# Output projection of a gated MLP as a stage of its own, with one level of Strassen's scheme over pairs of token tiles

## The chip, the cores and the metric

The kernel runs on one core of one Trainium2 chip. The metric is the device time of one execution in microseconds (us); the median of several runs is given, and one further execution was recorded by the hardware profiler. The engines are called PE (TensorE), DVE (VectorE), ACT (ScalarE), POOL (GpSimd) and SP (SyncE); PEld is TensorE's loading of weights.

## What is computed

One layer over 2048 tokens of 640 features: sliding-window attention with a residual, and then a gated MLP with a residual. The MLP is what matters here; with h the result of the attention part, it is

```python
F = w_in.shape[-1]; Fh = F // 2                      # F = 1728, Fh = 864
z = _gelu(jnp.einsum("bsd,df->bsf", _layernorm(h), w_in))
z1 = z[..., :Fh]
z2 = _layernorm(z[..., Fh:], axis=-1)
g = jnp.einsum("ts,bsf->btf", w_sp, z2) + b_sp[None, :, None]
h2 = h + jnp.einsum("bsf,fd->bsd", z1 * g, w_out)    # w_out is 864 x 640
```

The spatial gate `w_sp @ z2` multiplies a 2048 x 2048 matrix with 2048 x 864; the output projection multiplies 2048 x 864 with 864 x 640. All is float32 in and out.

## The kernel before

A token tile has 128 tokens, so there are 16 tiles. A feature row of 864 is seen as two halves of 432 (`HF`), or as seven blocks of 128 (`KF`; the seventh has 96); an output row of 640 as two halves of 320 (`HD`). Float32 accuracy comes from splitting each operand into a high and a low part (fp32r): `split` writes the high part by a copy on ACT (L140) and the low part by a subtraction on DVE (L141), and each product is three matmuls, high by high, high by low, low by high.

The stages follow each other: layer norm and QKV, attention, `wo` with the residual (h goes to `h_d`), z1 (`z_pair`, results to `z1_d`), the first half of z2, the first half of the spatial gate, the second half of z2, the second half of the gate, and within the latter the output projection.

The gate works on pairs of token tiles p and p+8 (`gate_pair`, L1076), as one level of Strassen's scheme (Winograd's form with shared sums): two tiles by two halves of the contracted tokens on one side, by two feature halves of 432 on the other. The seven products are called B11, T1, T2, B22, T3, B21, T4; each is 4 blocks by 3 matmuls of 432 columns (L1136), 84 in a pair. `first_gate` does it with the first half of the contracted tokens and stores the partial sums to `g_d`. `second_gate` (L1223) loads those back, adds the products (L797, `row<-g`) and then forms z1·(g+b) by one scalar_tensor_tensor a half tile (`gated`, L1237) in one of two buffers for z1, into which z1 was loaded from `z1_d` (L1240).

The output projection takes one tile at a time: `turn_y` transposes the gated tile in seven pieces on PE (L1190) into two PSUM banks, from where ACT and DVE split it into `y_sp`; `project` (L1196) multiplies with the split `w_out` (7 blocks by 3 by 2 halves = 42 matmuls of 320 columns, L1201); `final_half` adds h and stores. During `second_gate(p)` the two tiles of pair p-1 are done, behind the gate's products 0 to 3 (`turns`, `extra`); the last two tiles come after the loop (L1371 to L1378). `w_out` is loaded and split in `second_gate(0)` (`load_wout`, `put_wout`).

The order: `steps` is a list of (PE part, what follows it) and `at(n, f)` hangs a preparation on step n; `run` walks through them. That gives the order of the program and by it the dependences. From step 62 on (L1361) no order by hand holds any more, and a list scheduler sets the order of the instructions of each engine; it may move an instruction ahead of others of its engine. All DMAs are issued on the SP queue. In PSUM there are 8 banks, 4 under the tag "a" and 4 under "b" (`bank`, L790); a bank is used again once what reads it has run.

## Time and profile before

| | us |
|---|---|
| median of 3 runs | 1126.52 (1121.55 to 1129.52) |
| the profiled execution: span | 1124.0 |
| first pair of the second gate | 873 to 893 |
| other seven pairs, with the projection | 893 to 1113 |
| projection of the last tile, and the end | 1113 to 1124 |

The profiled execution has no time of its own beside its span; the span is 2.5 us below the median of the runs. In the views below, a row names an engine, the line of the kernel and the tiles (out<-in by their names in the program, without buffer numbers). The view of waits adds up, for each engine and line, how long the engine stood idle for which other engine's line; the chain of waits follows the work that ended last from the end of the execution back to its start; the view by windows gives the busy time of each engine in a stretch of time.

### The profile page before, as it was taken

The numbers are of one execution on the slowest core, as the hardware profiler recorded it, in microseconds if no ns is written. First come the engines' busy times: TensorE is split into PE (matmuls) and PEld (weight loads), VectorE is DVE, ScalarE is ACT, GpSimd is POOL, SyncE is SP. The second block draws the span as 40 slices with busy tenths as digits, with TensorE's granted clock in tenths as the row PEclk, the third lists the DMA queues.
The fourth block names the chain that finished last, engine by engine and source line by source line (L and its number), as shares of the span: only waits on it lengthen the run. The fifth ranks groups of instructions, "written<-read, shape, count | busy, mean of one in ns | idle before, by whom it ended". The sixth has DMA issues, their size and how long they took to land.

```text
span 1124.0 us, 28713 instructions
## 1 busy us (share of the span) xinstructions
PE 1089.4 (97%) x11139; PEld 980.3 (87%) x11139; DVE 752.8 (67%) x2070; ACT 567.5 (50%) x1155; POOL 319.6 (28%) x447
## 2 busy tenths in 40 slices
PE   8999999989999999999999999999999999999998
PEld 8998887657877777699899999999999899999998
DVE  6643444779988999588877678655358974556542
ACT  4444443248988899735566567434347521222210
POOL 4324446766766666723200011000001000000000
PEclk9999999989999999999999999999999999999999
DMA  7834567545555555689554522242251563444321
GB/s 256 283 113 135 171 186 248 183 157 181 179 179 172 177 178 165 170 249 311 218 195 167 182 91 76 75 134 90 104 171 57 180 209 119 124 148 148 98 87 60
DMA packets 87672, 180.57 MB, mean 161 GB/s; under 512 B 11440, under 2 KB 45760, under 8 KB 83648
## 3 DMA queue, kind: packets, MB, share of 16 engines
q1 hardware_dynamic: 87536, 178.74, 49.8%
q8 instruction: 87, 1.43, 0.5%
q14 instruction: 49, 0.40, 0.1%
HBM read 120.82 MB, written 57.88 MB: 159 GB/s over the span
## 4 chain that ended last, share of the span: by engine, by line
PE 72%; DMA 8%; ACT 7%; DVE 6%; issue 3%; POOL 2%; SPq 1%; DVEq 0%; POOLq 0%; ACTq 0%
PE g L1136 22%; PE out_ps L1201 8%; ACT pt L397 5%; PE pv L422 4%; PE zb L1028 4%; PE qk L568 3%; PE qk L569 3%; PE qk L570 3%; PE bank L341 3%; PE bank L394 3%; PE zx L976 2%; PE zv L976 2%; PE zy L976 1%; PE wo_ps L101 1%; DMA o_d<-ot 1%
## 5 line engine op out<-in xcount | busy, mean ns | idle before, releaser
L397 ACT ACTIVATE pt<-bank 128x384 f32<-128x384 f32 (+1 forms) x452 | 180.1, 478 | 26.4 <-PE bank L394 16.2
L803 ACT ACTIVATE aw<-fx 128x512 fp32r<-128x512 f32 (+2 forms) x160 | 93.7, 596 | 173.5 <-PE g L1136 120.7
L1136 PE MATMUL g<-zl,aw 128*128 128x432 f32 x768 | 171.0, 358 | 0.0
L351 DVE CUSTOM_DVE_ANT_0 junk<-bank,strip 128x288 bf16<-128x288 f32 x392 | 156.7, 454 | 16.3 <-PE bank L341 13.8
L1136 PEld LDWEIGHTS g<-zl,aw 128*128 128x128 f32 x768 | 143.6, 188 | 5.9
L422 PE MATMUL pv<-pt,v_sb 128*32 128x192 f32 (+3 forms) x1984 | 129.6, 323 | 6.2 <-ACT ot L438 3.8
L1136 PE MATMUL g<-ze,aw 128*128 128x432 f32 x576 | 134.0, 360 | 0.3 <-DVE row L797 0.2
L797 DVE TENSOR_TENSOR aw<-fx,aw 128x512 fp32r<-128x512 f32 (+2 forms) x160 | 102.7, 647 | 37.1 <-ACT aw L803 35.8
L1136 PEld LDWEIGHTS g<-ze,aw 128*128 128x128 f32 x576 | 107.0, 188 | 6.7 <-ACT aw L803 1.2
L401 POOL TENSOR_SCALAR_AFFINE_SELECT pt<-pt 128x512 f32<-128x512 f32 x128 | 83.9, 656 | 62.7 <-ACT pt L397 60.2
L394 PE MATMUL bank<-slot 123*32 123x288 bf16 (+7 forms) x1296 | 94.4, 276 | 4.9 <-ACT pt L397 3.5
L1201 PE MATMUL out_ps<-wout,y_sp 128*128 128x320 f32 (+1 forms) x630 | 96.2, 309 | 0.4 <-ACT y_sp L140 0.4
L341 PE MATMUL bank<-slot 120*32 120x288 bf16 (+6 forms) x1280 | 92.2, 277 | 3.6 <-issue 1.6
L1028 PE MATMUL zb<-win,aw 128*128 128x432 f32 x480 | 95.4, 359 | 0.0
L1201 PEld LDWEIGHTS out_ps<-wout,y_sp 128*128 128x128 f32 (+1 forms) x630 | 94.1, 188 | 1.2 <-ACT y_sp L140 0.7
L87 POOL TENSOR_TENSOR mvz<-mvz,half 128x1 f32<-128x1 f32 x16 | 10.1, 633 | 298.8 <-DVE mvz L86 296.8
L1028 PEld LDWEIGHTS zb<-win,aw 128*128 128x128 f32 x480 | 89.9, 187 | 5.0 <-ACT row L803 0.3
L422 PEld LDWEIGHTS pv<-pt,v_sb 128*32 128x32 f32 x1984 | 59.9, 110 | 18.1 <-issue 9.9
L797 DVE TENSOR_TENSOR row<-g,row 128x432 f32<-128x432 f32 x80 | 48.2, 604 | 37.8 <-PE g L1136 36.9
L394 PEld LDWEIGHTS <-slot 123*32 123x32 bf16 x1728 | 58.5, 97 | 15.3 <-issue 6.0
L404 POOL TENSOR_SCALAR_AFFINE_SELECT pt<-pt 128x512 f32<-128x512 f32 x112 | 71.4, 637 | 0.0
L351 DVE CUSTOM_DVE_ANT_0 junk<-bank,mask 128x384 bf16<-128x384 f32 (+2 forms) x120 | 51.7, 447 | 21.1 <-PE bank L345 15.8
(196 smaller groups left out, 2247.1 us busy)
## 6 DMA issues: line engine op xcount, KB each, us to landing
slot<-qk_d SPq DMA_DIRECT2D x144, 160.0 KB
fx<-wsp_in SPq DMA_DIRECT2D x32, 512.0 KB
qk_d<-sg SPq DMA_DIRECT2D x40, 384.0 KB
fx<-hn_d SPq DMA_DIRECT2D x32, 320.0 KB
o_d<-ot SPq DMA_DIRECT2D x64, 128.0 KB
xb<-qk_d SPq DMA_DIRECT2D x48, 160.0 KB
z_d<-row SPq DMA_DIRECT2D x16, 432.0 KB
g_d<-row SPq DMA_DIRECT2D x16, 432.0 KB
```

The lines of the kernel that those rows point to most:

```text
L341: nc.tensor.matmul(ps[32 * j:32 * j + 32, o:o + w], one(st, 120, 0, hh, q0, 32), k, start=True, stop=True, tile_position=(0, 32 * j))
L351: nc.vector.tensor_tensor_reduce(out=junk[:, :n], in0=ps[:, :n], in1=keep, scale=1.0, scalar=NEG, op0=OP.add, op1=OP.max, accum_out=m_cols ...
L394: nc.tensor.matmul(ps[32 * i:32 * i + 32, b + o:b + o + w], one(st, 123, 1, hh, k0, 32), q, start=True, stop=True, tile_position=(0, 32 * i))
L397: nc.scalar.activation(pt[:, hh, :n], ps[:, :n], AF.Exp, scale=SCALE)
L401: nc.gpsimd.affine_select(out=pt[:, :, :P], in_=pt[:, :, :P], pattern=[[0, 4], [1, P]], base=0, channel_multiplier=-1, compare_op=OP.is_ge ...
L404: nc.gpsimd.affine_select(out=pt[:, :, 256:], in_=pt[:, :, 256:], pattern=[[0, 4], [-1, P]], base=-1, channel_multiplier=1, compare_op=OP. ...
L422: nc.tensor.matmul(ps[32 * hh:32 * hh + 32, a - 512 * c:b - 512 * c], v_sb[:, kb, v0:v0 + 32], pt[:, hh, a - kb * P:b - kb * P], start=fir ...
L797: (eng or nc.vector).tensor_tensor(out=out, in0=a, in1=b, op=op)
L803: nc.scalar.activation(out, a, AF.Copy)
L1028: nc.tensor.matmul(b[0][:, :HF], a[t][:, x, kk], win2[0][:, y, kk, h * HF:(h + 1) * HF], start=kk + x + y == 0, stop=kk == KD - 1 and x == 1)
L1136: nc.tensor.matmul(ps, w[m][:, x, k], zc[k][m][:, y], start=start and k + x + y == 0, stop=stop and k == 3 and x == 1, skip_group_check=True)
L1201: nc.tensor.matmul(ps[j][:, :HD], src[:w, a, k, :], e1["wout"][:w, b, k, j * HD:(j + 1) * HD], start=(k == 0 and a + b == 0), stop=(k == K ...
```

## The change

The output projection becomes a stage behind the gate. `second_gate` stores each gated tile to a new DRAM tensor `y_d` (128 x 864 a tile), and `out_pair(q)`, called for eight pairs of tiles behind all of the gate, loads two tiles into `fx` and transposes them. Of the seven feature blocks six are taken as two halves of three, and with the two tiles and the two output halves they form one level of the same Strassen scheme: seven products of 3 blocks by 3 matmuls of 320 columns, 63 a pair. The seventh block (`wo6`, 96 rows) is done directly, 4 x 3 matmuls (`prod6`). Left operands go to `aw` for even pairs and to `zc[3]` for odd ones; the sums of them are formed from the transposes in PSUM (`sums`, `third`, `fourth`). The right operands are differences of `w_out`'s quarters, split into high and low: B11, T1, T2, B22 and B21 are prepared in `second_gate` 1 to 3 (`wout_steps`), the seventh block in 4, and T3 and T4 around the last gate pair, with subtractions on POOL, in buffers of z2 that are read no more (`wout_late`). Each product is added to h as it ends, 8 additions a pair in the place of 4. In line numbers of the kernel after the change, 142 and 798 are `split`'s and the additions' lines, 1139 the gate's matmul, 1263 the transpose, 1308 and 1314 the projection's matmuls, 1365 the gating.

```diff
+    y_d = dram.tile([NT, P, FH], F32, name="y_d")
...
-        e1["wout"] = p.tile([P, 2, KF, D], F32R, name="wout")
-        e1["y"] = p.tile([P, 2, KF, P], F32R, name="y_sp")
+        e1["w"] = {m: [p.tile([P, 2, HD], F32R, name=f"wo{m}_{k}") for k in range(3)] for m in (B11, T1, T2, B22, B21)}
+        for m, n in ((T3, B11), (T4, T1)):
+            e1["w"][m] = [zc[k][n][:, :, :HD] for k in range(3)]
+        e1["w6"] = p.tile([P, 2, D], F32R, name="wo6")
         e1["z1"] = [p.tile([P, FH], F32, name=f"z1_{n}") for n in range(2)]
-        e1["h"] = [p.tile([P, D], F32, name="hr"), rows[3][:, :D]]
+        e1["raw"] = [p.tile([P, D], F32, name="wo_raw"), rows[3][:, :D]]
...
-    def turn_y(n, dst):
...
-    def project(ps, js, src):
-        for k in range(KF):
-            w = min(P, FH - k * P)
-            for a, b in ((0, 0), (0, 1), (1, 0)):
-                for j in js:
-                    nc.tensor.matmul(ps[j][:, :HD], src[:w, a, k, :], e1["wout"][:w, b, k, j * HD:(j + 1) * HD],
-                                     start=(k == 0 and a + b == 0), stop=(k == KF - 1 and a == 1))
...
-    def final(n):
-        ps = [bank("b", f"out_ps{n}_{j}") for j in range(2)]
-        project(ps, range(2), e1["y"])
-        for j in range(2):
-            final_half(ps, n, j, j == 1)
...
+    def wout_steps(k):
+        w, (b11, b12, b21, b22) = e1["w"], [t[:, j * HD:(j + 1) * HD] for t in e1["raw"] for j in range(2)]
+
+        def hi(m, raw):
+            copy(w[m][k][:, 0], raw)
+
+        def lo(m, raw, eng=None):
+            minus(w[m][k][:, 1], raw, w[m][k][:, 0].bitcast(F32), eng)
+
+        def first():
+            lo(B11, b11)
+            minus(b11, b12, b11)
+            hi(T1, b11)
+
+        def third():
+            lo(B21, b21)
+            minus(b11, b22, b11)
+            hi(T2, b11)
+            hi(B22, b22)
+
+        return [lambda: hi(B11, b11), first, lambda: (lo(T1, b11), hi(B21, b21)), third,
+                lambda: (lo(T2, b11), lo(B22, b22))]
...
+    def wout_late(k):
+        w, (b11, b12, b21, b22) = e1["w"], [t[:, j * HD:(j + 1) * HD] for t in e1["raw"] for j in range(2)]
+        eng = nc.gpsimd
+        minus(b11, b12, b11, eng)
+        minus(b12, b22, b12, eng)
+        minus(b11, b22, b11, eng)
+        minus(b21, b21, b11, eng)
+        for m, raw in ((T3, b12), (T4, b21)):
+            split(w[m][k][:, 0], w[m][k][:, 1], raw, eng)
...
+    def out_pair(q):
...
+        def load_y():
+            for t in range(2):
+                nc.sync.dma_start(ys[t], y_d[tiles[t]])
...
+        def turn(t):
+            o[t] = [bank("b", f"yt{q}_{t}_{j}") for j in range(2)]
+            for k in range(KF):
+                w, j = min(P, FH - k * P), k // 3 - k // 6
+                c = (k - 3 * j) * P
+                nc.tensor.transpose(o[t][j][:w, c:c + P], ys[t][:, k * P:k * P + w], ident)
...
+        def early():
+            a11, a12, _ = parts(0)
+            put(B11, a11)
+            put(B21, a12)
+            put6(0)
+
+        def sums():
+            (a11, a12, _), (a21, a22, _) = parts(0), parts(1)
+            r, s1, s2 = opened()["raw"]
+            copy(r, a21)
+            plus(s1, a22, r)
+            minus(s2, s1, a11)
+            put(T2, s2)
+            put(T1, s1)
+
+        def third():
+            a11, a21 = parts(0)[0], parts(1)[0]
+            r = opened()["raw"][0]
+            minus(r, a11, r)
+            put(T3, r)
+
+        def fourth():
+            s2 = opened()["raw"][2]
+            minus(s2, parts(0)[1], s2)
+            put(B22, s2)
+            put6(1)
...
+        def prod(b, m, start, stop):
+            l, r = o["l"][m], e1["w"][m]
+            for k in range(3):
+                for x, y in ((0, 0), (0, 1), (1, 0)):
+                    nc.tensor.matmul(o[b][:, :HD], l[:, x, k * P:(k + 1) * P], r[k][:, y], start=start and k + x + y == 0,
+                                     stop=stop and k == 2 and x == 1, skip_group_check=True)
...
+        pe = [lambda: (new("x"), prod("x", B11, True, False)),
+              lambda: (new("y"), prod("y", B21, True, False), prod6("y", 0, 0, False)),
+              lambda: prod("x", T2, False, False),
+              lambda: (new("v"), prod("v", T1, True, False)),
+              lambda: prod("x", T3, False, False),
+              lambda: (prod("v", B22, False, False), prod6("v", 0, 1, False), prod6("y", 1, 1, True)),
+              lambda: (prod("x", T4, False, False), prod6("x", 1, 0, False))]
+        post = [lambda: add(0, 0, "x"), lambda: add(0, 0, "y"), lambda: add(0, 1, "x"), lambda: add(1, 1, "v"),
+                lambda: add(1, 1, "x"),
+                lambda: (add(0, 1, "v"), store(0), add(1, 1, "y"), *([store(1, 1, 2)] if last else [])),
+                lambda: (add(1, 0, "x"), store(1, 0, 1 if last else 2))]
+        steps.extend(zip(pe, post))
+        m = n0 - 7
+        at(m - (4 if even else 3), load_y)
+        at(m + 2, lambda: turn(0))
+        at(m + 3, lambda: (turn(1), early()))
+        at(m + 4, sums)
+        at(m + 5, third)
+        at(m + 6, fourth)
+        at(n0, lambda: put(T4, parts(1)[1]))
+        at(n0 - 2 if q else n0, load_h)
...
-        turns = (0, 1, 2, 3) if p > 1 else (0, 4, 4, 6)
-
-        def extra(m):
-            if p:
-                for x, f in zip(turns, (lambda: turn_y(i - 2, e1["y"]), lambda: final(i - 2),
-                                        lambda: turn_y(i - 1, e1["y"]), lambda: final(i - 1))):
-                    if x == m:
-                        f()
...
-        at(n0 + (turns[2] + 1 if p else 0), lambda: load_z(j))
+        at(n0 + (2 if p else 0), lambda: load_z(j))
...
+        for t in range(2):
+            at(n0 + 7 + t, lambda t=t: nc.sync.dma_start(y_d[p + 8 * t], e1["z1"][t]))
+        gate_pair(p, 1, [add(11), add(22), add(12), add(12), add(22), add(11), add(21)], lambda m: None)
+        if 1 <= p <= 3:
+            at(n0 - 2, lambda: wout_raw(p - 1))
+            for t in range(5):
+                at(n0 + 1 + t, lambda t=t: wout_steps(p - 1)[t]())
+        if p == 4:
+            at(n0 - 1, lambda: wout_raw(6, False))
+            at(n0 + 2, lambda: split(e1["w6"][:, 0], e1["w6"][:, 1], e1["raw"][0]))
+        if p == 7:
+            at(n0 - 4, lambda: wout_raw(0))
+            for k in range(3):
+                at(n0 + 2 + 2 * k, lambda k=k: (wout_late(k), wout_raw(k + 1) if k < 2 else None))
...
+    for p in range(8):
+        out_pair(p)
...
-    n = NT - 2
-    turn_y(n, e1["y"])
-    final(n)
-    turn_y(n + 1, y_sp2)
-    ps = [bank("b", f"out_l{j}") for j in range(2)]
-    for j in range(2):
-        project(ps, (j,), y_sp2)
-        final_half(ps, n + 1, j, 2)
```

The list scheduler sets what stands where. PE, in the middle of the old projection: `yt_ps11` are the transposes of tile 11, `out_ps11` its products, `g1_6` and `g1_7` the gate's products of pairs 6 and 7.

```order
L1190 MATMUL yt_ps11_0_15026<-ident_72,z1_1_13517 128x128 x4
L1190 MATMUL yt_ps11_4_15033<-ident_72,z1_1_13517 128x128 x2
L1190 MATMUL yt_ps11_4_15033<-ident_72,z1_1_13517 96x128
L1136 MATMUL g1_6_1_14952<-zl12_10081,aw_10090 128x432 x2
L1136 MATMUL g1_6_0_14918<-ze4_11050,aw_10090 128x432 x3
L1136 MATMUL g1_6_0_14918<-ze11_11057,aw_10090 128x432 x3
L1136 MATMUL g1_6_0_14918<-zl6_10075,aw_10090 128x432 x3
L1136 MATMUL g1_6_0_14918<-zl13_10082,aw_10090 128x432 x3
L1136 MATMUL g1_7_0_15164<-zl9_10078,aw_10090 128x432 x3
L1136 MATMUL g1_7_1_15197<-ze1_11047,aw_10090 128x432 x3
L1136 MATMUL g1_7_1_15197<-ze8_11054,aw_10090 128x432
L1201 MATMUL out_ps11_0_15058<-wout_13514,y_sp_13515 128x320
```

PE at the beginning of the new stage: `yt2` are the transposes of the third pair (pair 2), `out0` and `out1` the products of pairs 0 and 1.

```order
L1314 MATMUL out0_v_14701<-wo6_13530,aw_10091 128x320 x3
L1308 MATMUL out1_x_14773<-wo0_0_13515,zl9_10079 128x320 x3
L1308 MATMUL out1_x_14773<-wo0_1_13516,zl9_10079 128x320 x3
L1308 MATMUL out1_x_14773<-wo0_2_13517,zl9_10079 128x320 x3
L1263 MATMUL yt2_0_1_14799<-ident_73,fx_10092 128x128 x3
L1263 MATMUL yt2_0_1_14799<-ident_73,fx_10092 96x128
L1263 MATMUL yt2_1_0_14817<-ident_73,fx_10092 128x128 x3
L1263 MATMUL yt2_1_1_14818<-ident_73,fx_10092 128x128 x3
L1263 MATMUL yt2_1_1_14818<-ident_73,fx_10092 96x128
L1308 MATMUL out0_x_14639<-wo2_0_13521,aw_10091 128x320 x3
```

Transposes of a tile and its products stood between gate matmuls; now the transposes of one pair stand between the products of the two pairs before it, and no gate matmul is left between them.

DVE at the same places. Before, behind the transposes of tile 11:

```order
L797 TENSOR_TENSOR hr_13518<-out_ps10_0_14965,hr_13518 128x320
L797 TENSOR_TENSOR hr_13518<-out_ps10_1_14966,hr_13518 128x320
L141 TENSOR_TENSOR y_sp_13515<-yt_ps11_0_15026,y_sp_13515 128x512
L797 TENSOR_TENSOR row0_10085<-g1_6_1_14952,row0_10085 128x432
L141 TENSOR_TENSOR y_sp_13515<-yt_ps11_4_15033,y_sp_13515 128x256
L1237 SCALAR_TENSOR_TENSOR z1_0_13516<-row0_10085,bcol_77,z1_0_13516 128x432
L141 TENSOR_TENSOR y_sp_13515<-yt_ps11_4_15033,y_sp_13515 96x128
L797 TENSOR_TENSOR row1_10086<-g1_6_0_14918,row1_10086 128x432
L797 TENSOR_TENSOR aw_10090<-fx_10091,aw_10090 128x512
L797 TENSOR_TENSOR row2_10087<-g1_7_0_15164,row2_10087 128x432
L1237 SCALAR_TENSOR_TENSOR z1_1_13517<-row1_10086,bcol_77,z1_1_13517 128x432
```

After, at the end of the gate. The three rows ahead of these are the addition of the gate's last product (128x432) and two instructions of 128x384; `z1_0<-row2` is the gating of the last half tile.

```order
L1365 SCALAR_TENSOR_TENSOR z1_0_13531<-row2_10088,bcol_78,z1_0_13531 128x432
L142 TENSOR_TENSOR aw_10091<-yt2_0_0_14798,aw_10091 128x384
L798 TENSOR_TENSOR row0_10086<-row0_10086,yt1_0_0_14665 128x384
L798 TENSOR_TENSOR wo_raw_13533<-yt1_0_0_14665,wo_raw_13533 128x384
L142 TENSOR_TENSOR zl10_10080<-row0_10086,zl10_10080 128x384
L142 TENSOR_TENSOR zl5_10075<-yt1_1_1_14685,zl5_10075 96x128
L142 TENSOR_TENSOR zl4_10074<-yt1_0_1_14666,zl4_10074 96x128
L142 TENSOR_TENSOR zl11_10081<-row0_10086,zl11_10081 128x384
L142 TENSOR_TENSOR zl13_10083<-wo_raw_13533,zl13_10083 128x384
L142 TENSOR_TENSOR aw_10091<-yt2_0_1_14799,aw_10091 128x384
L798 TENSOR_TENSOR row0_10086<-yt1_0_1_14666,row0_10086 128x384
L142 TENSOR_TENSOR zl15_10085<-yt1_1_1_14685,zl15_10085 128x384
```

The splits of one tile stood between additions of the gate; now the splits and sums of pair 1 and the first splits of pair 2 stand in one row behind the last gating.

SP before, in one pair of the gate: the two z1 loads stand behind each other, and h is loaded and the output stored.

```order
L1240 DMA z1_0_13516<-z1_d_69 128x864
L1240 DMA z1_1_13517<-z1_d_69 128x864
L1221 DMA h2_out<-hr_13518 128x640
L1253 DMA row2_10087<-g_d_71 128x432
L1208 DMA hr_13518<-h_d_68 128x640
L1221 DMA h2_out<-row3_10088 128x640
L1208 DMA row3_10088<-h_d_68 128x640
L1253 DMA row2_10087<-g_d_71 128x432
L1088 DMA fx_10091<-wsp_in 128x1024
```

SP after, in one pair of the gate: `y_d<-z1_0` is the store of a gated tile.

```order
L1380 DMA y_d_72<-z1_1_13532 128x864
L1370 DMA row0_10086<-g_d_71 128x864
L1368 DMA z1_1_13532<-z1_d_69 128x864
L1372 DMA row2_10088<-g_d_71 128x432
L1380 DMA y_d_72<-z1_0_13531 128x864
L1372 DMA row2_10088<-g_d_71 128x432
L1368 DMA z1_0_13531<-z1_d_69 128x864
L1091 DMA fx_10092<-wsp_in 128x1024
L1372 DMA row1_10087<-g_d_71 128x432
L1380 DMA y_d_72<-z1_1_13532 128x864
```

A z1 load now stands behind the store from the same buffer, and loads of partial sums (`g_d`) and of `w_sp` stand behind it; the loads of h and the stores of the output are gone from here.

82 lines of the change are left out of this document (51 added, 31 removed).

## The prediction

> **What bounds the kernel now.** I read the page first: the span, and the engines' busy time.
>
> ```profile
> span 1124.0 us, 28713 instructions
> PE 1089.4 (97%) x11139; PEld 980.3 (87%) x11139; DVE 752.8 (67%) x2070; ACT 567.5 (50%) x1155; POOL 319.6 (28%) x447
> ```
>
> TensorE (PE) is busy for 97% of the span, but a share over the whole span is an average of stages. So I cut out the stretch that the change touches, in the view by windows; the columns after the window are its length, the busy time (with the number of instructions) of PE, weight load, DVE, ACT and POOL, the granted clock, the DMA share and the GB/s.
>
> ```profile
> 873.00:892.60 19.60, 17.21 (x86) 15.45 (x85) 18.42 (x35) 12.25 (x21) 1.06 (x3) 1.00 0.61 207
> 892.60:1112.70 220.10, 219.68 (x1322) 213.81 (x1323) 122.71 (x228) 46.16 (x92) 0.00 (x0) 1.00 0.41 128
> 1112.70:1124.00 11.30, 7.69 (x52) 7.02 (x50) 3.18 (x7) 1.15 (x3) 0.00 (x0) 1.00 0.16 59
> ```
>
> The first is the first pair of the second gate, the second the other pairs with the projection between them, the third the projection of the last tile. Over 220 us PE is idle for 0.4 us, at a clock of 1.00, while DVE is at 56%, ACT at 21% and POOL at nothing. What lies there costs its PE time and nothing else. The list of what PE waits for from 826 us on confirms it (total, times, longest, in us):
>
> ```profile
> PE yt_ps L1190 <- DVE z L1237: 2.2, 1, 2.2
> PE out_ps L1201 <- ACT y_sp L140: 0.4, 1, 0.4
> PE out_l L1201 <- ACT aw L140: 0.4, 1, 0.4
> PE g L1136 <- DVE row L797: 0.2, 1, 0.2
> ```
>
> The chain of waits gives prices (start, us, what):
>
> ```profile
> 710.46 113.01 PE g L1136 x576
> ...
> 824.48 5.20 DMA fx<-wsp_in
> ...
> 873.00 5.31 DMA hr<-w_out_in
> ...
> 887.80 2.88 DMA row<-g_d
> ...
> 1085.07 6.17 PE out_ps L1201 x42
> 1091.24 0.77 PE yt_ps L1190 x7
> ```
>
> A gate matmul of 432 columns takes 113.01/576 = 0.196 us, an output matmul of 320 columns 6.17/42 = 0.147, a transpose 0.77/7 = 0.11.
>
> **The change part by part.**
>
> *Matmuls.* A pair of tiles takes 7 products x 3 blocks x 3 = 63 matmuls and 4 x 3 = 12 for the seventh block: 75 for 84. Eight pairs save 72 x 0.147 = **10.6 us**. Gate matmuls (8 x 84) and transposes (8 x 14) stay as many. As PE ends last everywhere here, all of it is on the path. The Trainium skill, "TensorE: Matmul & The Clock Gate", section "Back-to-back issue gap", puts an isolated warm matmul of N columns at N/2.4 + 2.5 ns; for 320 that is 135.8 ns, 8% under the row, and the saving would be an estimated 9.8 us. The row decides.
>
> *The end.* The last two tiles no longer stand one behind the other; the last pair's transposes and splits lie in the pair before it. So both waits of 0.4 for ACT go: **-0.8**. The last add and the store behind it stay.
>
> *The start of the second gate.* PE's 2.4 us of idle time (2.2 + 0.2) hang on DVE, busy 18.42 of 19.60 us there. The transposes that wait leave, and with them three splits of w_out. But by the new order PE needs for pair 0's product T3 that DVE has added an earlier product and freed its bank, and from 879.5 us there are 22 DVE instructions up to that add. The timeline of DVE gives what one costs from start to start:
>
> ```profile
> 891.26 0.69 DVE L797 TENSOR_TENSOR aw<-fx,aw 128x512 fp32r<-128x512 f32 x1
> 891.86 0.66 DVE L1237 SCALAR_TENSOR_TENSOR z<-row,bcol,z 128x432 f32<-128x432 f32 x1
> 892.44 0.60 DVE L797 TENSOR_TENSOR row<-g,row 128x432 f32<-128x432 f32 x1
> 892.96 0.68 DVE L797 TENSOR_TENSOR aw<-tmp,aw 128x512 fp32r<-128x512 f32 x1
> 893.56 0.60 DVE L797 TENSOR_TENSOR row<-g,row 128x432 f32<-128x432 f32 x1
> ...
> 895.79 0.81 DVE L141 TENSOR_TENSOR wout<-hr,wout 128x640 fp32r<-128x640 f32 x1
> 896.53 0.82 DVE L141 TENSOR_TENSOR wout<-row,wout 128x640 fp32r<-128x640 f32 x1
> ...
> 1112.94 0.89 DVE L797 TENSOR_TENSOR hr<-out_ps,hr 128x320 f32<-128x320 f32 x2 [4.83 <-PE out_ps L1201]
> ```
>
> So 512 columns step by 0.60 us, the gating by 0.58, 432 by 0.52, 640 by 0.74, and the second of two of 320 adds 0.40; in line with these I take 384 at 0.465 and 128 at 0.20 (estimates). 22 x 0.56 = 12.4 ends at 891.9, and PE's 84 matmuls from 873 end at 889.5: the same 2.4 us again, in another place. **0**; the bound is -2.4.
>
> *Gate pairs without the projection.* PE 84 x 0.196 = 16.5 us. DVE: 11 of 512, 7 adds, 4 gatings = 6.6 + 3.6 + 2.3 = 12.5; in pairs 1 to 3 w_out's 7 pieces of 320 bring it to 15.3, 93% of PE's time, against 56% now. Per pair hidden, with 1.2 us to spare: **0**. ACT gets 5 of 320 there. In DMA a pair loads w_sp, the partial sums and z1, and now stores y: about 3.7 MB in 16.5 us, 225 GB/s (some 265 with w_out in pairs 1 to 3), where the first window moved 207 at a share of 0.61: that fits.
>
> *The trip through y_d.* Gated z1 (432 KB a tile) is now stored, and only then may the next tile of z1 load into its buffer. SP issues in program order, so behind a load that waits stand the loads of the next partial sums and of w_sp. What the queue of SP waits for today:
>
> ```profile
> SPq L1240 <- PE yt_ps L1190: 44.1, 9, 11.1
> ...
> SPq L1208 <- DMA h_out<-row: 17.1, 7, 4.5
> SPq L1208 <- DMA h_out<-hr: 17.0, 7, 3.8
> ```
>
> z1's load waits up to 11.1 us now and PE doesn't notice. A load behind a store of the same buffer, the next two rows, waits 34.1/14 = 2.4 us in the mean, 4.5 at most, and loads land in 2.9 to 5.3 us (the chain's rows): 5.3 to 9.8 us a trip. Between the two gatings of a tile lie two steps and one instruction, 2 x 2.35 + 0.66 = 5.4 us; of the 16.5 us of a pair 11.1 are left. It fits, narrowly at the upper bound: **0**. The Trainium skill, "DMA: Bandwidth & Descriptors", section "Anatomy of one DMA — SWDGE (gpsimd) path", has about 2.0 us fixed and bytes/436 GB/s, and adds that a write to HBM may complete late; 432 KB would be an estimated 3.0 us, a trip 6.0, inside the rows' span.
>
> *Preparing w_out.* The differences T3 and T4 come around gate pair 7 on POOL, idle there: 6 instructions a block, 18 in all.
>
> ```profile
> L551 POOL TENSOR_TENSOR wol<-woraw,woh 128x640 fp32r<-128x640 f32 x5 | 7.9, 1581 | 11.9 <-ACT woh L550 6.8 <-DMA xt<-x_in 2.6 <-issue 2.5
> ```
>
> Half of that size is about 0.8 us, so 18 x 0.8 = 14.4 us beside the pair's 16.5, with reloads of w_out (5.3) between; by this they end some 13 us before out pair 0 multiplies by T3. **0**.
>
> *Output pairs.* PE 75 x 0.147 + 14 x 0.11 = 12.6 us. DVE: 7 splits and 4 sums of 384, 2 of 128, 8 adds of 320 = 5.1 + 0.4 + 3.2 = 8.7; there were 4 adds a pair. ACT copies 8 times 384 and twice 128:
>
> ```profile
> L397 ACT ACTIVATE pt<-bank 128x384 f32<-128x384 f32 x396 | 164.1, 499 | 21.9 <-PE bank L394 12.2 <-POOL sg L592 4.2 <-PE bank L341 2.7
> ```
>
> 8 x 0.5 + 2 x 0.3 (an estimate) = 4.6 us. By throughput all is hidden. By order it isn't, as transposes need free banks, and banks come free when DVE has read them:
>
> (i) At the border pair 1's y loads into `fx`, where the last raw weights of the gate stand, so it can go only when ACT and DVE have split them, and behind the stores on SP. Followed along both orders, 0 to 1.8 us of its landing (2.9 to 5.3) reach PE; I take **0.7**, nearer to the covered end.
>
> (ii) From pair 1 to 2: behind the gate's last product DVE has its add, 11 instructions of 384, one gating and 2 of 128 (the last of them in the rows shown above) before the banks of yt2_1_0 and yt2_1_1 are free: 0.52 + 5.1 + 0.58 + 0.4 = 6.6 us. PE has in that time 7 transposes, 21 matmuls and 4 transposes: 0.77 + 3.1 + 0.44 = 4.3. PE waits **2.3**.
>
> (iii) The six handovers after it have only DVE's 8.7 us against 12.6, and no gate's backlog: 0 to 0.6 each, the longest being one more DVE instruction; together **1.5**.
>
> New waits 0.7 + 2.3 + 1.5 = 4.5 us; bounds 0, and 8 x 2.3 = 18.4 if each handover is like (ii).
>
> *Sum.* 1124.0 - 10.6 - 0.8 + 4.5 = 1117.1 us of span. The median of the runs shown is 1126.5, 2.5 above the profiled span: **1119.6 us**, 0.6% less.
>
> **The rivals.**
>
> *Faster, no new waits.* The scheduler has put the transposes far enough ahead, and the 2.4 us at the start go too: 1124.0 - 10.6 - 0.8 + 2.5 = 1115.1 with the old start, 1112.7 without it. For it: PE idle 0.4 of 220 us today with the same kind of handover. Against: 6.6 against 4.3 above. Chance 0.22.
>
> *Each handover waits.* All eight pairs wait like (ii): 1115.1 + 18.4 = 1133.5. For it: one set of 4 banks holds two tiles' transposes whole, until the last sum is read. Against: 8.7 us of DVE in 12.6. Chance 0.13.
>
> *Slower: the trip through y_d decides.* If store and load come late, as 207 GB/s goes to over 225, a trip half as long again as the upper bound is 14.7 us, 3.6 more than the 11.1 free. The gating is late by that, so the store, so the next load: 7 x 3.6 = 25 us, 1115.1 + 4.5 + 25 = 1145. It decides from 11.1 us a trip. For it: the SP queue holds loads of w_sp behind it, and 0.61 of the DMA share was the densest pair. Against: today's 4.5 at most. The Trainium skill's page "DMA: Bandwidth & Descriptors", same section, bears it out so far as it says that writes to HBM can complete late; no run here shows it yet. Chance 0.10.
>
> *It isn't the work that was meant*: excluded by count, 600 matmuls for 672.
>
> **How the numbers follow.** The forecast has 0.55. Some 1% (11 us) is what measurements of this kernel can tell from no change: faster means under 1115.3, slower over 1137.8. Under 1115.3 lie the faster rival, nearly all, and the low edge of the forecast, where new waits stay under 0.2: 0.22 + 0.02 = 0.24. Over it: 0.10, and 0.02 of the handovers where DVE is later than (ii). Same: 0.64. The range from 1111 (1112.7, and the 1.6 by which the measured median may fall nearer to the span than 2.5) to 1134 (the third case whole) leaves out the last rival and some 0.05 at its edges.
>
> **What would show it.** 600 output matmuls at 0.147 us, behind one another; the gate's pairs 16.5 us each, ending near 1007; the SP queue waiting for y_d's stores at z1's loads, with PE not waiting for `gated`; one wait of some 2 us of a transpose for DVE at the border, and short ones later; DVE at some 90% in pairs 1 to 3. The forecast is wrong if PE waits in the gate's pairs, or if the granted clock falls below 1.00 behind such a wait.

## The result and the profile after

The kernel after the change takes 1132.58 us in the median (1128.49 to 1136.47, 9 runs), against 1126.52 us before: a ratio of 1.0053, 95% interval 1.0028 to 1.0077. It is half a per cent slower. The forecast was 1119.6 us, with a range from 1111 to 1134: the time lies on the other side of no change. That it still lies in the range is luck, as the range reached so far up for a rival (all handovers of the output stage wait) that did not come. The profiled execution, which is one of the nine (1135.04 us):

```profile
span 1133.3 us, 28831 instructions
PE 1086.2 (96%) x11067; PEld 970.7 (86%) x11067; DVE 798.8 (70%) x2173; ACT 587.7 (52%) x1202; POOL 338.2 (30%) x465
```

72 matmuls are gone, and PE is busy for 3.2 us less and not for 10.6; the span is 9.3 us longer. Ahead of the second gate the change touches nothing, but that part varies by itself from one execution to the next. The first matmul of the second gate, before and after:

```profile
873.01 1.34 PE L1136 MATMUL g<-ze,aw 128*128 128x432 f32 x6
```

```profile
874.23 1.34 PE L1139 MATMUL g<-ze,aw 128*128 128x432 f32 x6
```

So 1.2 of the 9.3 us were lost ahead of it; from this matmul to the end it is 251.0 us before and 259.1 after. By windows, from the start of the second gate (columns as in the prediction):

```profile
873.00:893.00 20.00, 18.73 (x91) 16.48 (x90) 18.09 (x37) 11.88 (x23) 2.10 (x4) 1.00 0.44 150
893.00:1010.00 117.00, 107.32 (x539) 99.19 (x540) 89.13 (x157) 32.46 (x60) 8.32 (x7) 1.00 0.66 217
1010.00:1133.30 123.30, 114.49 (x763) 111.53 (x761) 84.22 (x184) 36.67 (x85) 10.62 (x11) 0.98 0.52 168
```

In the gate PE now stands for 9.7 of 117 us, where it stood for 0.4 of 220. What PE waits for from 826 us on:

```profile
PE g L1139 <- DVE row L798: 9.2, 6, 2.3
PE yt L1263 <- DVE row L798: 2.1, 1, 2.1
PE g L1139 <- ACT aw L804: 1.8, 2, 1.1
PE yt L1263 <- DMA fx<-y_d: 1.0, 1, 1.0
PE out_y L1308 <- DVE row L798: 0.9, 1, 0.9
PE g L1139 <- DVE aw L798: 0.6, 1, 0.6
...
```

The first row is the result: gate products wait for DVE's additions (`row<-g`). And DVE waits, between 893 and 1010 us:

```profile
DVE fx L798 <- DMA fx<-wsp_in: 7.3, 3, 3.3
DVE row L798 <- DMA row<-g_d: 6.8, 6, 2.3
DVE tmp L798 <- DMA fx<-wsp_in: 6.2, 4, 2.1
```

20 us of DVE's time go by at the head of its queue, before loads of w_sp and of the partial sums (with 0.9 us for z1 it is 21.2); an addition behind them waits too, and with it PE. The shares of the chain of waits in the same 117 us, before and after, say it in two lines:

```profile
by line: PE g L1136 55.3%; PE out_ps L1201 39.6%; PE yt_ps L1190 5.1%
```

```profile
by line: DMA fx<-wsp_in 30.6%; DVE aw L798 12.3%; DMA row<-g_d 12.0%; DVE row L798 9.5%; DMA y_d<-z 7.3%; DVE z L1365 7.2%; issue 6.7%; DMA row<-w_out_in 5.8%; DVE fx L798 3.4%; DVE wo L798 2.7%; ACT aw L804 1.7%; DVE wo_raw L798 0.7%; DVE 
```

Before, the chain ran over PE alone; after, over loads and what they release, and no line of PE is among those listed. A piece of it, in order of time:

```profile
964.04 0.59 DVE z L1365
...
964.65 4.50 DMA y_d<-z
...
969.17 0.32 SPq L1368
...
969.54 7.54 DMA fx<-wsp_in
...
977.78 0.67 DVE z L1365
```

A store to y_d lands, SP may issue the z1 load that waited for it, and only then the w_sp load behind that, which takes 7.5 us. That is the rival of the trip through y_d, and it was what I tested first.

### The profile page after: what moved, and what is told of

Read it like the earlier page. It is cut to its first block, busy times and chain, and to the rows that moved or that the text cites. A ratio compares the mean times of both kernels' runs of the same rounds, so it can differ in the third digit from the quotient of the medians.

```text
span 1133.3 us, 28831 instructions
## 1 busy us (share of the span) xinstructions
PE 1086.2 (96%) x11067; PEld 970.7 (86%) x11067; DVE 798.8 (70%) x2173; ACT 587.7 (52%) x1202; POOL 338.2 (30%) x465
## 4 chain that ended last, share of the span: by engine, by line
PE 65%; DMA 13%; DVE 7%; ACT 7%; POOL 3%; issue 3%; SPq 1%; DVEq 0%; POOLq 0%; ACTq 0%
PE g L1139 12%; PE zb L1031 8%; PE pv L423 5%; ACT pt L398 5%; PE out_x L1308 4%; PE bank L342 3%; PE qk L569 3%; PE qk L571 3%; PE qk L570 3%; PE bank L395 3%; DMA fx<-wsp_in 3%; PE zx L979 2%; PE zv L979 2%; DMA row<-g_d 2%; PE out_v L1308 2%
## 5 line engine op out<-in xcount | busy, mean ns | idle before, releaser
L398 ACT ACTIVATE pt<-bank 128x384 f32<-128x384 f32 (+1 forms) x452 | 180.2, 477 | 26.4 <-PE bank L395 15.3
L395 PE MATMUL bank<-slot 123*32 123x288 bf16 (+8 forms) x1296 | 95.9, 276 | 4.6 <-ACT pt L398 3.7
L593 POOL TENSOR_TENSOR sg<-rest,sg 128x512 bf16<-128x512 f32 x40 | 46.7, 1167 | 57.0 <-ACT sg L592 46.3
L342 PEld LDWEIGHTS <-slot 120*32 120x32 bf16 x1440 | 51.0, 96 | 12.9 <-issue 5.4
```

Of the source, the lines that this page charges most:

```text
L342: nc.tensor.matmul(ps[32 * j:32 * j + 32, o:o + w], one(st, 120, 0, hh, q0, 32), k, start=True, stop=True, tile_position=(0, 32 * j))
L395: nc.tensor.matmul(ps[32 * i:32 * i + 32, b + o:b + o + w], one(st, 123, 1, hh, k0, 32), q, start=True, stop=True, tile_position=(0, 32 * i))
L398: nc.scalar.activation(pt[:, hh, :n], ps[:, :n], AF.Exp, scale=SCALE)
```

## The experiments

Three theories stood. **T**, the trip: z1's loads wait for y_d's stores and hold up what is behind them on SP. **B**, bytes: more is moved than arrives in time. **D**, DVE: w_out's preparation fills it. A fourth, **C**, came with the first results: the projection's matmuls between the gate's products had been the cover for lateness that was there all along. Gains and losses are medians against the 1132.58 us of the kernel after the change; ratios are against the kernel before, with 95% intervals. Two such intervals together leave some 4 to 5 us open: by this e7 and e15 below are faster than the kernel after the change, e3, e6, e9, e10 and e12 slower, e2 and e11 at the edge; a gain of 2 to 4 us by itself shows nothing.

**T, B and D: take out the stores, move the issues, relieve DVE.** e1 leaves out the stores; e2 moves the z1 loads, e3 the stores too, to POOL's queue; e4 moves the subtractions of `wout_steps` to POOL.

```diff
-            at(n0 + 7 + t, lambda t=t: nc.sync.dma_start(y_d[p + 8 * t], e1["z1"][t]))       # e1
-            nc.sync.dma_start(e1["z1"][n % 2], z1_d[tile_of(n)])                             # e2, e3
+            nc.gpsimd.dma_start(e1["z1"][n % 2], z1_d[tile_of(n)])
+            at(n0 + 7 + t, lambda t=t: nc.gpsimd.dma_start(y_d[p + 8 * t], e1["z1"][t]))     # e3
-            minus(b11, b12, b11)                                                             # e4
+            minus(b11, b12, b11, nc.gpsimd)
```

> The kernel after the change, without the 16 stores of gated tiles to y_d; the output stage loads the ungated z1 in their place, so the gating is left out of the result. All matmuls, transposes and loads are as many as before. Theory T (a z1 load waits at the head of SP's queue for the landing of the store from its buffer, and the w_sp and partial-sum loads behind it come late): the waits of PE for DVE between 893 and 1010 us, 9.2 us of which 2.3 are the old one at the start, fall to 2 to 4 us, and the time by 5 to 8 us, to some 1125 us. Rival B (the DMA engines move more than the transfers' due times allow, whatever their order): the stores are 0.9 of 3.7 MB of a pair, so the waits fall to 5 to 7 us, the time by 2 to 4. Rival D (DVE, at over 90% in pairs 1 to 3): no change.

> The kernel after the change with only the loads of z1 issued from POOL's queue, which has nothing to do in the gate; the stores to y_d stay on SP and the z1 loads still wait for them, but nothing stands behind a waiting load any more. T: if the order on SP is what makes w_sp and the partial sums late, the waits of PE in the gate fall to 2 to 4 us and the time by 5 to 8 us; if it is the trip of z1 itself that is late, the waits stay at 9. B: no change, as the bytes are the same. D: no change.

> As e2, with the stores to y_d on POOL's queue too. The stores wait on SP for the gating today (23.3 us in 14 times), so they also hold up what is behind them. T: as e2 or up to 3 us better. B and D: no change against the kernel after the change.

> The kernel after the change with the seven subtractions of 320 columns in each of gate pairs 1 to 3 that prepare w_out on POOL in the place of DVE (DVE has 2.8 us less to do in each). D: the waits of PE for DVE between 897 and 950 us (0.9, 1.8, 1.0 and 2.2 us in the profile) go, and the time falls by 4 to 6 us. T and B: these waits stay within 2 us in sum, as those behind 950 us show that pairs without the preparation wait too; time within 2 us.

Measured: e1 1130.47 us (1.0036, 1.0011 to 1.0060); e2 1140.10 (1.0097, 1.0061 to 1.0134); e3 1144.87 (1.0142, 1.0091 to 1.0192); e4 1129.72 (1.0030, 1.0008 to 1.0053). Without any store 2.1 us came back, not T's 5 to 8, and the gate's waits between 893 and 1010 us stay at 9.0 us (9.8); but this profile is of e1's slowest execution (1136.99 us). With z1's loads away from SP, another wait stands at the head of its queue, between 893 and 1010 us in e2:

```profile
SPq L1372 <- DVE z L1365: 31.5, 7, 8.6
SPq L1380 <- DVE z L1365: 28.2, 11, 5.7
SPq L1091 <- DVE aw L798: 20.9, 10, 7.4
```

These are the partial sums, which wait for a row that the gating still reads, the stores, and w_sp itself. Nothing here speaks for T as the main cause, and e5, which has no y_d, settles that. D's 4 to 6 us were not seen (2.9 in e4). B's 2 to 4 us are what e1 gave, so B stays open.

**C: the gate alone, in the kernel before.** e5 is the kernel before without the output projection (no transposes, splits or matmuls of it; h is stored as it is), so with no y_d and w_out prepared in pair 0 only.

```diff
 def project(ps, js, src):
+    return
 def turn_y(n, dst):
+    return
-        plus(ht[:, c], ps[j][:, :HD], ht[:, c])
```

> The kernel before without the transposes, the splits of y and the matmuls of the output projection, so that h alone is stored; the second gate stands there with nothing between its products, and with no trip through y_d and no w_out preparation beyond pair 0. Theory C (lost cover: a gate product needs the addition of the product two ahead of it in the same bank, DVE stops in its own queue at late loads, and the projection's matmuls between the products were what hid it): PE waits for DVE in the gate as in the kernel after the change, 6 us or more in sum between 893 us and the gate's end. Theory T (the stores to y_d and what they hold up): PE waits under 3 us there, the gate ends near 873 + 1 + 132 + 3 = 1009 us.

It was executed once: span 1028.0 us. PE's waits from 873 us on, and the windows:

```profile
PE g L1136 <- DVE row L797: 10.7, 8, 2.9
...
```

```profile
873.00:893.00 20.00, 17.30 (x74) 14.36 (x72) 16.27 (x30) 11.82 (x20) 1.76 (x3) 0.91 0.49 168
893.00:1010.00 117.00, 109.62 (x524) 103.10 (x525) 82.69 (x140) 27.85 (x45) 0.00 (x0) 0.94 0.70 238
```

The same additions, waits as long (12.1 us in all), and nothing of the change in it but the lost projection. The projection's own work on PE is 672 x 0.147 + 112 x 0.11 = 111.1 us, but from the gate's first matmul to the end e5 is only 251.0 - 157.3 = 93.7 us shorter: 17.4 us come back. So its leaving is the cause, as C has it. Part of the lateness was in the trace of before already; among DVE's waits between 873 and 1124 us, 10.0 of them for loads, stood there

```profile
DVE tmp L797 <- DMA fx<-wsp_in: 7.3, 4, 2.8
```

and PE did not notice, since 42 matmuls and seven transposes (6.9 us) of a tile lay between the products. The rest is new: between 893 and 1010 us alone DVE waits 21.2 us for loads in the kernel after the change, and 21.2 in e5. Without the projection the gate's loads fall due in about half the time (a DMA share of 0.41 over the seven pairs before, 0.66 after, 0.70 in e5). So the projection's leaving does two things at once, it takes the cover away and it crowds the loads, and no run here separates their shares. At two of PE's three longest waits in the gate of the kernel after the change the DMA engines are full, at the third they are empty (the last two columns: DMA share and GB/s):

```profile
894.00:895.00 1.00, 0.00 (x0) 0.00 (x0) 1.00 (x4) 0.00 (x0) 0.00 (x0) 1.00 0.00 0
...
916.00:917.00 1.00, 0.00 (x0) 0.00 (x0) 1.00 (x3) 0.63 (x1) 0.00 (x0) 1.00 1.02 409
...
948.00:949.00 1.00, 0.00 (x0) 0.00 (x0) 0.26 (x1) 0.00 (x0) 0.92 (x3) 1.00 1.03 396
```

**Which loads: leave them out.** e7 loads w_sp, e8 the partial sums, for the first two pairs of the second gate only; e17 is e5 with e7's edit, e18 is e5 with both. The later values are then others than the reference's; the instructions of the engines stay.

```diff
+        if not c or p < 2:                                        # e7, e17, e18
             at(n0 - 11 if p != 1 else n0 - 10, load)
+        if p < 2:                                                 # e8, e18
             at(n0 - (3 if p else 1), lambda: nc.sync.dma_start(gi, g_d[p]))
```

> The kernel after the change with w_sp loaded for the first two pairs of the second gate alone; the later pairs work on what stands in the buffers, so the gate's values are wrong. All instructions of the engines stay. If arrivals of w_sp stop DVE and with it PE: the waits of PE in the gate fall from 9.8 to 3 to 4 us (the old one at the start and what partial sums cause), the time to 1125 or less. If the partial sums or z1's trip are enough by themselves: 6 us or more stay.

> The kernel after the change with the partial sums g_d loaded for the first two pairs of the second gate alone; later pairs add to what stands in the three row buffers, so values are wrong. Instructions of the engines stay. It takes 12 times two or three loads out of SP's queue that wait there for the gating (19.3 us). If the row buffers' loads are the cause: the waits of PE in the gate fall from 9.8 to 3 to 4 us; if w_sp's arrivals are, to 6 or more.

> e5 (the kernel before without its output projection) with w_sp loaded for the first two pairs of the second gate alone. There is no y_d and no preparation of w_out beyond pair 0. By theory C the late w_sp loads are the greater part of what the missing cover lays open: the waits of PE in the gate fall from 12 to 2 to 5 us, and the clock stays at 1.00 for most of it; the gate ends near 1012 us, the span is near 1015. If w_sp has no part in it, the span stays near 1028.

> e17 with the partial sums, too, loaded for the first two pairs alone (later pairs add to what stands in the rows). Every instruction of PE, DVE and ACT of e5 stays; of the gate's loads only z1 and h are left. e17 missed: without w_sp the waits stayed at 10.7 us, now behind partial sums. If the gate alone waits because DVE, in order, stops at whichever load is late, and nothing lies between the products to hide it: with both gone PE's waits fall to 4 us or less behind 893 us, the span to 1013 to 1018. If DVE's own work or the distance of two products is too short even without late loads: waits of 7 us or more stay, span 1022 or more.

e7 takes 1126.11 us (0.9997, 0.9977 to 1.0016), 6.5 less, as fast as before; e8 1129.17 (1.0033, 1.0013 to 1.0053). PE's waits in e7 from 870 us on, the border's among them:

```profile
PE g L1140 <- DVE row L798: 2.9, 3, 2.3
PE g L1140 <- ACT aw L804: 2.4, 3, 1.0
PE out_x L1309 <- DVE row L798: 2.3, 1, 2.3
PE yt L1264 <- DVE row L798: 2.1, 1, 2.1
PE out_y L1309 <- DVE row L798: 1.1, 1, 1.1
```

So w_sp is the larger part there by the times; e8's 3.4 us are within the noise. The gate's waits don't tell them apart: between 893 and 1010 us they fall from 9.8 to 2.6 us in e7 and to 3.7 in e8. In the gate alone the spans, 1025.6 us in e17 against e5's 1028.0, hide the same, because the part ahead of the gate took another time in each execution. The first matmul of the second gate in e5, e17 and e18:

```profile
870.75 1.34 PE L1136 MATMUL g<-ze,aw 128*128 128x432 f32 x6
```

```profile
875.58 1.34 PE L1137 MATMUL g<-ze,aw 128*128 128x432 f32 x6
```

```profile
868.16 1.34 PE L1137 MATMUL g<-ze,aw 128*128 128x432 f32 x6
```

From there to the end e5 takes 157.3 us, e17 150.0 and e18 147.6: w_sp is 7.3 of the 9.7 us that both loads give, by one execution of each. e17 still missed what was expected of it, and its gain came by another way: PE waited nearly as long as in e5 (10.7 us against 12.1), and what fell is the cost of the lowered clock (last section), from 8.0 us to 2.5. DVE now stood before the partial sums and once before z1:

```profile
PE g L1137 <- DVE row L797: 10.2, 9, 3.9
...
```

```profile
DVE row L797 <- DMA row<-g_d: 5.7, 6, 2.3
DVE z L1241 <- DMA z<-z_d: 5.4, 1, 5.4
```

With both gone (e18) the span is 1015.8 us, 12.2 under e5 and in the range expected of C, 2.6 of it by the earlier start; 5.6 us of waits remain behind 893 us, 4.1 of them one wait, and the next load was late in its turn:

```profile
DVE z L1241 <- DMA z<-z_d: 10.4, 2, 9.2
```

w_sp is the largest, but no single load is the cause. Whichever is late stops DVE, and when it is taken away the next comes forward. As a load that is left out takes its bytes with it, these runs don't tell late issues from full DMA engines.

**Put cover back, and other ways to be on time.** e12 adds 12 matmuls of 432 columns that nobody reads to each of the gate pairs 1 to 7. e6 issues the second gate's w_sp loads from POOL, e13 from ACT; e9 computes the sums of w_sp's pieces on POOL, e10 is e9 with e4.

```diff
+            if c and m in (T1, T3):                                                      # e12
+                d = bank("b", f"d{p}_{m}")[:, :HF]
+                for k in range(2):
+                    piece(d, m, k, True, True)
-                nc.sync.dma_start(view(fx, f0 + o, 8, P), wsp[t, :, 8 * c:8 * c + 8, :])
+                (nc.gpsimd if c else nc.sync).dma_start(view(fx, f0 + o, 8, P), wsp[t, :, 8 * c:8 * c + 8, :])   # e6; e13: nc.scalar
-            plus(s1, a21, a22)
+            plus(s1, a21, a22, eng=nc.gpsimd if c and p else None)                       # e9, e10; so the other three
```

> The kernel after the change with 12 more matmuls of 432 columns in each of the gate pairs 1 to 7 (six behind product T1, six behind T3, into a bank that nobody reads), 84 in all, 16.5 us of PE. They stand where the projection's matmuls stood, with nothing that they wait for. By theory C they hide what DVE and the loads are late by: PE's waits in the gate fall from 9.8 to under 3 us, the half-speed clock goes, and the time grows by 5 to 10 us and not by 16.5. If PE's waits are nothing that work in between can hide (each product late by a fixed chain of its own), the time grows by 14 us or more.

> The kernel after the change with the loads of w_sp of the second gate issued from POOL's queue, where no waiting load stands ahead of them. If the order on SP's queue makes w_sp late (DVE waits 13.5 us for it between 893 and 1010 us), that wait falls under 7 us and the time falls by 4 us or more; if the queue isn't it, the time stays within 2 us or gets worse.

> The kernel after the change with the second gate's w_sp loads issued from ACT's queue, behind ACT's own splits of the same buffer and ahead of nothing of SP's. If SP's order makes w_sp late, and POOL's queue was slow of itself in e6: DVE's waits for w_sp fall from 13.5 to under 7 us and the time by 3 to 6 us. If the lateness comes from the transfers and the free buffer, no gain, and up to 5 us of loss as ACT stands behind a waiting issue.

> The kernel after the change with the four sums of w_sp's pieces in each pair of the second gate (from pair 1 on) on POOL in the place of DVE. These are the instructions in which DVE stops for late w_sp loads (13.5 us between 893 and 1010 us). If it is DVE's standing still in its queue that delays the additions for which PE waits (theory C), DVE's waits for w_sp go, PE's waits in the gate fall from 9.8 to 4 to 6 us and the time by 3 to 5 us. If the lateness of the splits themselves is what counts (the left operands are late for PE whoever makes them), PE waits as long, for aw in the place of row, and POOL's slower sums make it 0 to 4 us worse.

> e9 and e4 together: the sums of w_sp and w_out's preparation in pairs 1 to 3 on POOL. By theory C the gains add up: 5 to 8 us under the kernel after the change, 1125 to 1128 us; by the other, the same as e4 or worse.

e12: 1143.88 us (1.0153, 1.0118 to 1.0188), 11.3 us more for 16.5 us of added matmuls. With some 5 us open this lies between what was expected of C (5 to 10) and of its rival (14 or more) and settles neither; the gate's waits between 893 and 1010 us went from 9.8 to 6.4, not under 3. Twelve matmuls in two places of a pair are a thinner cover than 42 and seven transposes for each of its two tiles; a cover as thick as the old one was not tried. The others missed: e6 1137.45 us (1.0105, 1.0077 to 1.0132), e13 1132.04 (1.0050, 1.0022 to 1.0078), e9 1139.80 (1.0115, 1.0088 to 1.0142), e10 1140.42 (1.0131, 1.0110 to 1.0152). e9 shows why taking the stop away from DVE doesn't help; DVE's and ACT's waits between 893 and 1010 us:

```profile
DVE aw L798 <- ACT aw L804: 16.5, 10, 2.9
```

```profile
ACT aw L804 <- POOL fx L798: 36.3, 9, 7.7
```

POOL needs 1.3 us for a sum of 512 columns that DVE steps through in 0.6, ACT waits for POOL's sums, DVE for ACT's copies: the same additions are late at the end of a longer chain.

**The border.** e11 leaves out the late preparation of T3 and T4 (the output stage multiplies by T1 and T2 in their place); e14 does the first block's load and subtractions in pair 5; e15 is e14 with e4; e16 is e15 with the trip through y_d by halves of a tile.

```diff
-        for m, n in ((T3, B11), (T4, T1)):                                        # e11
-            e1["w"][m] = [zc[k][n][:, :, :HD] for k in range(3)]
+        for m, n in ((T3, T1), (T4, T2)):
+            e1["w"][m] = e1["w"][n]
...
-            for k in range(3):
-                at(n0 + 2 + 2 * k, lambda k=k: (wout_late(k), wout_raw(k + 1) if k < 2 else None))
...
+        if p == 5:                                                                # e14, e15, e16
+            at(n0, lambda: wout_raw(0))
+            at(n0 + 4, lambda: wout_late(0, splits=False))
         if p == 7:
-            at(n0 - 4, lambda: wout_raw(0))                                       # e11, e14, e15, e16
-            at(n0 + 7 + t, lambda t=t: nc.sync.dma_start(y_d[p + 8 * t], e1["z1"][t]))   # e16
+            at(n0 + 5 + x, lambda t=t, c=slice(hf * HF, (hf + 1) * HF):
+               nc.sync.dma_start(y_d[p + 8 * t][:, c], e1["z1"][t][:, c]))
```

> The kernel after the change without the late preparation of T3 and T4 around gate pair 7 (six loads of w_out, 18 instructions of POOL, 6 copies of ACT): the output stage multiplies by T1's and T2's tiles in their place, so its values are wrong and its matmuls are as many. If this chain (loads, POOL, then the load of h into the row that it has used) is what PE waits for at the border (5.3 us between 1010 and 1040 us, and 3.4 us at half clock behind it), these waits fall to 2 us or less and the time by 4 to 6 us. If it is the backlog of DVE behind the gate's last product (step ii of the prediction), 2 to 3 us of wait stay and the time falls by 1 to 2 us.

> The kernel after the change with the first of the three blocks of T3 and T4 loaded and subtracted already in gate pair 5 (only its splits stay in pair 7), so that the late chain is one load and four POOL instructions shorter, some 8 us. If that chain is late for the output stage (as e11 points to): waits between 1010 and 1045 us from 5.3 to 3 to 4 us, time 2 to 4 us less. If e11's gain came from the bytes that it left out: no change.

> e14 and e4 together. If both gains are real, 1126 to 1128 us, as fast as before; if e4's and e14's differences were only the spread between executions, 1130 to 1133.

> e15 with the trip through y_d cut in halves: each gated half of a tile (216 KB) is stored right behind its gating, and z1 is loaded by halves behind it. In e15 a store and the load behind it take 6.2 + 4.4 = 10.6 us in the chain of waits, at the limit of 11.1 us. If that trip is still a cause: 2 to 4 us less than e15, 1124 to 1125, just faster than before. If not, or if twice as many DMAs on SP cost what they save: 1127 or more.

e11: 1127.63 us (1.0018, 0.9993 to 1.0042), 5.0 less; e14 1129.02 (1.0025, 1.0003 to 1.0047); e15 1127.30 (1.0005, 0.9986 to 1.0023); e16 1134.93 (1.0079, 1.0052 to 1.0106). In e11 this wait between 1010 and 1045 us stays to the tenth, so it is DVE's backlog behind the gate's last product and not the late chain (the other waits there fall from 3.2 to 1.5 us):

```profile
PE yt L1263 <- DVE row L798: 2.1, 1, 2.1
```

One caution comes from e11. Its program is the same as that of the kernel after the change until gate pair 6, and yet its waits for the additions between 896 and 965 us are 2.5 us against 5.9. Between 893 and 1010 us PE waits 3.6 us in e11's profile and 5.4 in e14's, where it waits 9.8 in that of the kernel after the change. One profile's sum of such waits varies by several us, and the verdicts go by the medians. e15 puts its two gains together and is as fast as the kernel before; e16 is 7.6 us slower than e15, so the halves save nothing; no version here was faster than the kernel before.

## Why the prediction was wrong

By its own steps, from the forecast's 1117.1 us of span to 1133.3, 16.2 us:

- **Matmuls, right.** Nine matmuls of 320 columns take 1.32 us in the chain of the output stage, 0.147 each, and there are 72 less. The two waits of the old end went too, as said.

```profile
1070.43 1.32 PE out_x L1308 x9
```

- **Gate pairs without the projection, wrong: this is the step that failed.** I put DVE's 12.5 to 15.3 us against PE's 16.5 and called it hidden, by throughput, at a cost of 0, and I let the loads fit by throughput too. A gate product adds onto a bank from which DVE must first have read the product before it in that bank. In the program's order for pairs 1 to 7, 25 of the 35 such successions have 12 to 28 matmuls between them, mostly one or two products, at the prediction's prices an estimated 2.2 to 4.7 us; in the kernel before, the middle one of the 35 has 9.3. So what DVE had was not 16.5 us a pair but mostly under 5 us a product, and it stops in order at each late load, for 21.2 us in 117. The waits cost 9.8 - 2.3 = 7.5 us (the 2.3 being the old wait of the start). I had costed the projection as work on the path, and never as the cover of the gate; the question of what is late next when it goes was asked only of the output stage. Between the waits the gate's matmuls were slower as well, by 4.1 us, which I put down to restarts behind the waits: the view by windows has them at 124.06 us for 612, where 612 x 0.196 = 120.0.

```profile
873.00:1010.00 137.00, 124.06 (x612) 113.55 (x612) 1.00 0.63 207
```

- **The start, right but for 0.8.** The 2.3 us stand at 895 us, in the place that the order gave, and 0.9 us were added ahead of it.
- **The border, right in kind, too small.** Step (ii), 2.3 us of DVE's backlog, measured 2.1. With (i) I had 3.0; the waits sum to 5.3, +2.3. The preparation on POOL, put at 18 x 0.8 = 14.4 us and done some 13 us ahead, took 18.9 us and ended only at 1027.6, waiting for its reloads. No wait of PE names it, though; leaving it out gives 5.0 us (e11), starting it earlier 3.6 (e14), with some 4 us open on both, so that it costs something is likely and not shown.
- **The six handovers, right.** PE waits for nothing behind 1045 us; I had 1.5 and a lower bound of 0.
- **The clock, not in the sum.** It was named only as what would make the forecast wrong, and it fell behind the border's wait: 1.7 us (last section).
- **Ahead of the gate, chance.** The 1.2 us by which the gate began later.

That is 7.5 + 4.1 + 0.8 + 2.3 - 1.5 + 1.7 + 1.2 = 16.1 of the 16.2 us, for this one execution; in others the waits differ by several us (e11's caution). By the medians the miss is 13.0 us: the profiled execution took 1135.04 us, 1.7 above its span and 2.5 above the median of the nine, where the forecast had set the median 2.5 above the span.

**The rivals.** The trip through y_d had the right sign and the wrong condition: in e15's chain it took 10.6 us, near the bound of 11.1 that I had set, but without any store (e1) only 2.1 us came back, which is within the noise.

```profile
906.19 6.19 DMA y_d<-z
...
912.40 4.42 DMA z<-z_d
```

The Trainium skill, "DMA: Bandwidth & Descriptors", section "Anatomy of one DMA — SWDGE (gpsimd) path", from which I had estimated 6.0 us a trip, gives its fit for DMAs issued from POOL, where the kernel's are issued on SP, and warns of the late completion of writes to HBM. The rows don't agree with the 6.0. That the write is what made it late they don't show: in the kernel after the change two stores to y_d took 4.05 and 4.50 us, and loads of w_sp up to 7.65. The rival of waiting handovers did not come.

**What stays open.** Whether the loads are late for their issue (SP's queue in order) or for their transfers was not separated: moving the issue to ACT (e13) changed nothing that can be measured, and in e5 and in the kernel after the change the gate's DMA share is 0.70 and 0.66 in the mean and 1.0 at some of the waits, while in e18 it is 0.45. Nor was the lost cover separated from the crowding of the loads, and the preparation's cost at the border is not settled.

## What to carry to other kernels

Before work is moved out from between dependent steps, look up in the trace which waits of the other engines it has been hiding: DVE's waits for loads that PE does not notice are a price that appears when the cover goes, and the loads that remain crowd into less time. An engine's share of the time says nothing about that; what counts is how long after a product its consumer may be late, and here that was mostly one or two products. Taking one late load away brings the next one forward, so ask for all of them at once. And compare single executions from the start of the stage that was changed: what lies ahead of it differed by up to 8.7 us here between executions (868.2 to 876.9 us).

## What the runs showed that I had not expected

The granted clock falls behind waits shorter than I had looked for. At the border (windows of 1 us, PE alone and the clock matter):

```profile
1037.00:1038.00 1.00, 0.00 (x0) 0.00 (x0) 1.00 (x3) 0.30 (x2) 0.00 (x0) 1.00 0.98 350
...
1040.00:1041.00 1.00, 1.00 (x6) 1.00 (x5) 1.00 (x3) 0.00 (x0) 0.00 (x0) 0.50 0.70 233
...
1043.00:1044.00 1.00, 1.00 (x7) 1.00 (x7) 1.00 (x4) 0.84 (x2) 0.00 (x0) 0.79 0.00 0
```

Behind a wait of 2.07 us, seven transposes and a second wait of 0.22, PE ran at half the clock for 3.4 us, which costs 1.7. In e5 a wait of 2.69 did the same to the six matmuls behind it (2.53 us), while a wait of 2.34 in the kernel after the change did not (1.44 us for six). Earlier in e5 four waits of 0.18 to 0.58 us within 4 us were enough, the last of them 0.19:

```profile
880.27 2.53 PE L1136 MATMUL g<-ze,aw 128*128 128x432 f32 x6 [0.19 <-DVE row L797]
...
894.31 2.53 PE L1136 MATMUL g<-ze,aw 128*128 128x432 f32 x6 [2.69 <-DVE row L797]
```

```profile
895.11 1.44 PE L1139 MATMUL g<-ze,aw 128*128 128x432 f32 x6 [2.34 <-DVE row L798]
```

The Trainium skill, "TensorE: Matmul & The Clock Gate", section "What's actually happening", has the clock go down after at least one idle window of about 3.4 us; in these rows less was enough, 2.69 us in one piece or 2.07 and 0.22, or four short waits; where the limit lies they don't show. Summed up from 1-us windows between 873 and 1071 us (1024 in e5 and e17), the lowered clock cost 1.7 us in the kernel after the change, 6.0 in e1's profile, 8.0 in e5's and 2.5 in e17's. It makes the price of such waits uneven: e5 and e17 wait nearly as long, and most of the difference between them is the clock.
